# A fused spectral filter and expert layer: sums accumulated in HBM, statistics on ScalarE, and a fixed table of priorities

## The chip, the cores and the metric

The kernel runs on one core of one Trainium2 chip. The metric is the device time of one execution in microseconds (us), lower is better. The engines are named as in the profile: PE (TensorE, matrix products; PEld is its weight load), DVE (VectorE), ACT (ScalarE), POOL (GpSimd), and SP (SyncE), which here issues DMAs.

## What is computed

x has 2048 rows of 576 values. The result is the sum of x and of two branches over its layer norm:

```python
xn = layernorm(x)                                  # per row, eps 1e-5
A  = irfft2(rfft2(xn) * (w_r + 1j * w_i))          # 2-D transform, filter, back
q  = einsum("nd,dhc->nhc", xn, w_q)                # 32 heads, 2 x 128 per head
s1, s2 = q[..., :128] @ k1.T, q[..., 128:] @ k2.T  # 8 scores each
e  = 8 * argmax(s1) + argmax(s2)                   # one of 64 experts per head
B  = sum over heads of gelu(xn . u[e]) * v[e]      # top 1, so its softmax is 1
out = x + A + B
```

## The kernel before

**Tiles.** x is read as 16 tiles of 128 rows; tile t holds the rows n with n mod 16 = t. All matrix products run on PE. Inputs that need more than 16 bits are split into a high and a low 16-bit half and multiplied three times (high by high, high by low, low by high).

**Stages**, in the order in which the program records them:

- `ln` (L631) takes each row's mean and variance: two `bn_stats` of 288 values and one `bn_aggr` per tile on DVE, then the inverse root for a batch of 2 or 4 tiles.
- `folds` (L652) adds and subtracts mirrored halves of the rows (POOL and DVE), and `dft128` (L670) transforms over the 128 rows on PE. ACT copies PSUM as the high half, DVE subtracts for the low half.
- `fold_part` (L753) multiplies the keys into w_q, streamed from HBM in 32 loads of 576 KB through five buffers (tag `w`). `fold_scale` (L773) finds the largest result and `fold_end` (L780) transposes, scales and splits. Only then can the scores be computed.
- For each of 16 frequency groups: `load_w` and `load_s16` load the filter and small transforms, `w_scale` (L734) finds a scale for the filter, `d_fwd` (L897), `s_fwd`, `s_mul` and `s_inv` (L959) transform forward, multiply by the filter and transform back.
- For each of 8 pairs of tiles: `x_t` normalises and transposes x (a transposing DMA), `scores` (L819) computes 512 columns of scores, `route` (L846) and `combine` (L866) find each head's best expert on DVE and build the coefficients (`CAT`).
- For each of 16 tiles: `d_inv` (L990) does the last inverse transform on PE; ACT copies one half out of PSUM, DVE makes a sum and a difference of the halves, POOL puts the row together. `fin` (L1011) does the last product over the rows and the product with the experts' values into one PSUM tile; DVE scales it and adds x, which `load_x` (L540) loaded for two tiles at a time, and SP stores it.

**A maximum over partitions** is `allmax` (L615): PE transposes the column, DVE reduces, DVE puts the maxima on a diagonal (`mxd`), PE multiplies a matrix of ones with the diagonal, DVE clamps from below. It is called for the experts' matrices, for the folded weights and in each `w_scale`.

**The order of the work** is set by a planner in the kernel itself (L226 on). The stages only record operations, each with an estimated duration and its dependencies. The planner first goes backward from the end to get each operation's remaining path (`backward`, L330), then forward in time (`forward`, L350): on each engine it picks, of those that are ready, the one with the highest priority, and it also assigns PSUM banks. Ten such rounds are followed by a search of 1500 tries, in which each stage's priority is shifted at random and the best forecast is kept (`issue`, L443). `bias` values keep early work ahead. Only then are the instructions issued, all of them from one line:

```python
        for i in order:
            for fn, args, kw in ops[i].calls:
                fn(*[x.place() if isinstance(x, _Ps) else x for x in args],
```

That is why every row of the profile has L487; the rows are told apart by the names of their tiles. Each engine runs its own instructions in this fixed order and waits on semaphores for the others. SP's queue is also in order: a load that waits for its buffer holds up what stands behind it. `place` turns a bank number into an address.

Names in the profile: `banks` is PSUM; `Rs`, `A` and `yl` belong to the column transforms; `w` with `KP` to the weight fold; `mm__90` holds the maxima of the folded weights; `wx`, `Wt` and `wa` belong to the filter's scale; `AB` and `ABL` are the spectra; `MU` and `MUL` are the folded weights as the scores use them; `t`, `yh`, `A` and `w` name shared buffers, which the tail uses for the halves, for ACT's copy, for the assembled row and for x.

Of the kernel before, what the change touches and what calls it, by code (L numbers as in the profile page):

```python
# [10 lines left out]
F32 = mybir.dt.float32  # L11
# [124 lines left out]
TRIES, SEED = 1500, 2  # L136
# [87 lines left out]
class _Plan:  # L224
# [7 lines left out]
    def cost(self, eng, m, out, ins, kw):  # L232
# [4 lines left out]
        if eng == "sync":  # L237
            return out.shape[0] * n * size_of(out.dtype) / 400.0 + (2500 if kw.get("transpose") else 0), self.land
# [11 lines left out]
        if eng == "scalar":  # L250
            return (95 if ins[0].space == PSUM else 130) + 0.75 * n + 80 * ptr + 270 * ("accum_out" in kw), 180.0
        if eng == "gpsimd":
# [13 lines left out]
    def add(self, eng, fn, m, args, kw):  # L266
# [7 lines left out]
        port = eng == "gpsimd" and len(ins) > 0 or eng == "vector" and out.space != PSUM and (  # L274
# [75 lines left out]
    def forward(self, prio):  # L350
# [50 lines left out]
        best, stale = dict.fromkeys(free), set(free)  # L401
        while len(order) < len(ops):
# [25 lines left out]
            for v in o.tiles:  # L428
                left[v] -= 1
                end[v] = max(end[v], free[e] + o.lat)  # L430
                if not left[v]:
                    free_at[slot[v]:slot[v] + v.banks] = [end[v]] * v.banks
                    used[v.kind] -= 1
                    stale.add("tensor")
            for k, lat in o.after:
                ready[k] = max(ready[k], free[e] + lat)
# [6 lines left out]
    def issue(self):  # L443
# [16 lines left out]
        for _ in range(ROUNDS):  # L460
# [3 lines left out]
            if best is None or got[0] < best[0]:  # L464
                best = got
                cur = got[0], tail, np.zeros(self.stage + 1)
        rng = np.random.default_rng(SEED)
        for k in range(TRIES):
            f = 1 - k / TRIES
            tail, shift = cur[1], cur[2].copy()  # L470
            pick = rng.random(len(shift)) < (0.02, 0.05, 0.15)[rng.integers(3)]
            shift[pick] += rng.normal(0, 800 + 4000 * f, pick.sum())
            more = 400 * f * f * rng.exponential()
            if k % 40 == 39:
                tail, shift, more = self.backward(got[3]), cur[2], 300
            new = self.forward([t + o.bias + shift[o.stage] for t, o in zip(tail, ops)])
            if new[0] <= cur[0] + more:
                cur, got = (new[0], tail, shift), new
                if new[0] < best[0]:
                    best = new  # L480
# [18 lines left out]
def _body(ctx, tc, nc, plan, a, out):  # L499
# [52 lines left out]
    plan.land = 5600.0  # L552
# [62 lines left out]
    def allmax(src, k, dst):  # L615
# [532 lines left out]
```

## Time and profile before

| | |
|---|---|
| median of 3 runs | 236.74 us (236.53 to 237.49) |
| the profiled execution's own time | 237.5 us |
| its span, from the first to the last instruction | 235.6 us |
| mean granted TensorE clock | 0.986 of full speed |
| moved by DMA | 48.15 MB, 204 GB/s over the span |
| HBM read, written | 38.33 MB, 4.72 MB |

How to read the rows in this document. A row of the busy times gives, for each engine, microseconds in which it worked and the number of instructions; a row of a stretch starts with its limits and length, and ends with the granted clock, the share of time in which the DMA engines were busy and the GB/s. A row of a group names engine, operation, the tile written and the tiles read, the shapes, the count; behind the first bar stand the group's busy time in us and the mean of one instruction in ns, behind the second the idle time just before them and what ended it. In the rows of one tile three durations stand for shortest, median and longest (ns), then the first and last start. A row of the chain gives start, duration, and what ran, on the path that ended last. A DMA row gives count, size and the median us from issue to landing. A row of waits gives us in total, times and the longest.

### The profile page before, as it was taken

To read this page: it belongs to the slowest core of one execution; us is meant where nothing else is said; L and a number is where in the kernel's file an instruction comes from. 1 tells how busy PE (TensorE), PEld (TensorE's weight loads), DVE (VectorE), ACT (ScalarE), POOL (GpSimd) and SP (SyncE) were. 2 spreads that over 40 slices of the span, in tenths; PEclk is the share of its full clock that TensorE was granted. 3 is DMA by queue.
4 is the path that set the end of the run, shared out by engine and by line. 5 is a ranking of instruction groups with operands and counts; after the bars stand their busy time and mean duration, and the time that the engine had idled before them with its cause. 6 is when DMAs were issued, how large, how long until landed. Compare 5 with 4: busy or idle time off the path is not lost.

```text
span 235.6 us, 5937 instructions
## 1 busy us (share of the span) xinstructions
PE 200.0 (85%) x2271; PEld 135.8 (58%) x2271; DVE 204.3 (87%) x446; ACT 125.9 (53%) x287; POOL 134.4 (57%) x183
## 2 busy tenths in 40 slices
PE   0466888998999877899988979689999999999893
PEld 0454657776566545774454566265546778767661
DVE  2789999995999679976499999989999999968992
ACT  2232658989789599989635665256432121223120
POOL 2978768984264446736228886275813746545340
PEclk9997999999999999999999999979999999999999
DMA  6999999999999998466525561330521357662175
GB/s 211 401 403 415 362 334 375 406 349 373 284 338 374 392 251 148 106 164 59 110 53 122 115 134 38 79 59 3 100 59 46 99 156 253 198 203 100 50 245 208
DMA packets 34252, 48.15 MB, mean 204 GB/s; under 512 B 20784, under 2 KB 23088, under 8 KB 33840
## 3 DMA queue, kind: packets, MB, share of 16 engines
q1 hardware_dynamic: 34224, 47.77, 64.7%
q8 instruction: 18, 0.29, 0.6%
q14 instruction: 10, 0.08, 0.1%
HBM read 38.33 MB, written 4.72 MB: 183 GB/s over the span
## 4 chain that ended last, share of the span: by engine, by line
DVE 45%; PE 29%; ACT 9%; issue 8%; DMA 7%; POOL 1%; DVEq 0%; ACTq 0%; POOLq 0%
PE banks L487 29%; DVE w L487 9%; DVE t L487 8%; DVE AB L487 5%; DVE A L487 3%; DVE st L487 3%; DMA Wt<-in_W_dram 3%; DMA w<-in_x_dram 3%; DVE v L487 2%; DVE cw L487 2%; ACT AB L487 2%; DVE mx L487 2%; DVE ABL L487 2%; DMA XN<-in_x_dram 2%; DVE rr L487 2%
## 5 line engine op out<-in xcount | busy, mean ns | idle before, releaser
L487 POOL TENSOR_TENSOR A<-t 128x145 f32<-128x145 f32 (+3 forms) x56 | 38.4, 706 | 18.9 <-DVE t L487 12.2
L487 PE MATMUL banks<-MU,xT 128*128 128x512 f16 x192 | 46.0, 380 | 0.0
L487 PE MATMUL banks<-c,AB 128*128 128x145 f16 (+1 forms) x384 | 35.6, 228 | 0.7 <-DVE AB L487 0.7
L487 PEld LDWEIGHTS <-AB 128*128 128x128 f16 x384 | 31.6, 121 | 6.7 <-issue 4.3
L487 PE MATMUL banks<-Rs,A 128*128 128x128 f32 x128 | 20.5, 310 | 16.1 <-ACT Rs L487 11.8
L487 POOL TENSOR_TENSOR y<-t,t 128x289 f32<-128x289 f32 x32 | 21.7, 700 | 21.2 <-DVE t L487 20.8
L487 PEld LDWEIGHTS <-xT 128*128 128x128 f16 x224 | 19.8, 97 | 23.7 <-issue 4.1
L487 POOL TENSOR_TENSOR yh<-y,yh 128x578 f16<-128x578 f32 x16 | 20.6, 1285 | 16.7 <-ACT yh L487 12.9
L487 PEld LDWEIGHTS banks<-Rs,A 128*128 128x128 f32 x128 | 17.7, 214 | 21.1 <-ACT Rs L487 14.1
L487 POOL TENSOR_TENSOR t<-XN 128x289 f32<-128x289 f32 x32 | 24.5, 782 | 8.2 <-DMA XN<-in_x_dram 3.8
L487 DVE TENSOR_TENSOR AB<-banks,AB 128x512 f16<-128x512 f32 x32 | 21.6, 676 | 5.2 <-ACT AB L487 2.7
L487 DVE SCALAR_TENSOR_TENSOR t<-banks,wx,Wt 128x578 f32<-128x578 f32 x32 | 24.9, 807 | 0.4 <-PE banks L487 0.3
L487 POOL TENSOR_TENSOR hl<-XN,hl 128x576 f16<-128x576 f32 x16 | 20.0, 1254 | 8.0 <-ACT hl L487 8.0
L487 PE MATMUL banks<-c,ABL 99*128 99x289 f16 (+1 forms) x64 | 18.7, 292 | 5.6 <-DVE t L487 2.7
L487 ACT ACTIVATE yh<-banks,sc 128x290 f32<-128x290 f32 x16 | 8.0, 503 | 27.9 <-PE banks L487 23.9
L487 PE MATMUL banks<-A,c 128*128 128x288 f32 x64 | 21.6, 419 | 0.5 <-DVE t L487 0.5
L487 PE MATMUL banks<-w,KP 128*32 128x288 f32 x256 | 21.2, 428 | 0.0
L487 ACT ACTIVATE ABL<-banks 99x256 f16<-99x256 f32 x32 | 12.1, 378 | 16.6 <-PE banks L487 15.8
L487 ACT ACTIVATE AB<-banks 128x512 f16<-128x512 f32 x32 | 18.9, 590 | 0.1
L487 PE MATMUL banks<-s,yh 64*128 64x128 f16 x384 | 14.5, 222 | 4.9 <-ACT yh L487 1.9
L487 DVE TENSOR_TENSOR ABL<-banks,ABL 33x256 f16<-33x256 f32 x32 | 13.0, 405 | 6.3 <-ACT ABL L487 3.2
L487 PEld LDWEIGHTS <-yh 64*128 64x128 f16 x384 | 11.6, 97 | 9.6 <-issue 3.5
(104 smaller groups left out, 416.5 us busy)
## 6 DMA issues: line engine op xcount, KB each, us to landing
w<-in_wq_dram SPq DMA_DIRECT2D x32, 576.0 KB, 6.2
Wt<-in_W_dram SPq DMA_DIRECT2D x16, 289.0 KB, 5.4
w<-in_x_dram SPq DMA_DIRECT2D x8, 576.0 KB, 4.3
out_dram<-w SPq DMA_DIRECT2D x16, 288.0 KB, 2.7
XN<-in_x_dram SPq DMA_DIRECT2D x3, 1282.0 KB, 12.7
s<-in_s_dram SPq DMA_DIRECT2D x16, 192.0 KB, 3.1
XN<-in_x_dram SPq DMA_DIRECT2D x2, 641.0 KB, 5.0
c<-in_c_dram SPq DMA_DIRECT2D x1, 868.5 KB, 7.5
```

What stands on the lines that cost most here:

```text
L487: fn(*[x.place() if isinstance(x, _Ps) else x for x in args], **{k: x.place() if isinstance(x, _Ps) else x for k, x in kw.items()})
```

## The change

Four things are changed together, and the order of all instructions with them.

1. **The table.** The 1500 tries are dropped. A table `SHIFT` of one number per stage is written into the kernel and added to the priorities before one last forward pass. Some of the planner's estimates differ: loads early in the program count 3000 ns to landing where it was 5600, transposing DMAs 1200; a DMA issued from POOL is known; a queue of SP that is long busy adds 2600 ns; stages of the frequency groups get a small bias of 1e4.
2. **Maxima.** In `allmax` the diagonal is gone: the matmul takes the maxima, repeated along the free dimension with stride zero, as the stationary operand and the identity as the moving one. A factor can be multiplied in the clamp, which removes a DVE multiply in `w_scale` and in `fold_scale`.
3. **Statistics.** For tiles 5, 7, 9, 11, 13 and 15, `ln` takes them on ACT: one pass with an accumulator gives the negative mean (scaled), a second the mean square of the difference; POOL scales the mean.
4. **The tail.** For tiles 4, 5, 8 and 9, `d_inv` copies both halves out of PSUM on ACT, and POOL makes the difference that DVE made. For tiles 2, 3, 6 and 7 x isn't loaded: two DMAs on SP copy it from HBM to the output in HBM, `fin` lets ACT scale the PSUM tile into SBUF, and a DMA issued from POOL adds that to the output. In the new order the two copies stand among the last third of the loads of w_q.

```diff
-TRIES, SEED = 1500, 2
+SHIFT = (
+    4944, 32508, -18408, -5252, -68789, 83522, -16944, 5194, 4161, -48778, 60478, -11552, -28309,
...
+)
...
-        rng = np.random.default_rng(SEED)
-        for k in range(TRIES):
...
+        best = self.forward([t + o.bias + SHIFT[o.stage] for t, o in zip(cur[1], ops)])
...
+            lag = 0.0
+            if e == "sync":
+                if t0 > full[1]:
+                    full[0] = t0
+                full[1] = free[e] + 300
+                lag = 2600.0 if t0 - full[0] > 1500 else 0.0
...
-    plan.land = 5600.0
+    plan.land = 3000.0
...
-    def allmax(src, k, dst):
+    def allmax(src, k, dst, up=None):
...
-        dg = T([4, 4], F32, "mxd", 4)
-        V.tensor_scalar(dg[:k, :k], idn[:k, :k], m[:k, 0:1], None, op0=OP.mult)
-        P.matmul(p[:, 1, :k], ones[:k, :], dg[:k, :k], start=True, stop=True)
-        V.tensor_scalar(dst, p[:, 1, :k], 1e-10, None, op0=OP.max)
+        P.matmul(p[:, 1, :k], m[:k, 0:1].to_broadcast([k, 128]), idn[:k, :k], start=True, stop=True)
+        if up is None:
+            V.tensor_scalar(dst, p[:, 1, :k], 1e-10, None, op0=OP.max)
+        else:
+            V.tensor_scalar(dst, p[:, 1, :k], 1e-10, up, op0=OP.max, op1=OP.mult)
...
+    SA = (5,7,9,11,13,15)
...
+            if t + i in SA:
+                j, b = T([128, D], BF, "wa", 1), rr[:, 3, t + i:t + i + 1]
+                A.activation(j, XN[:, t + i, 64:64 + D], AF.Copy, scale=-1.0 / 13824, accum_out=b)
+                A.activation(j, XN[:, t + i, 64:64 + D], AF.Square, scale=1.0 / 24, bias=b, accum_out=mv[:, i, 1:2])
+                G.tensor_scalar(mv[:, i, 0:1], b, -24.0, None, op0=OP.mult)
+                continue
...
-        allmax(wm[:, g:g + n], n, wx[:, 0, g:g + n])
+        allmax(wm[:, g:g + n], n, wx[:, 0, g:g + n], 4096.0)
         V.reciprocal(wx[:, 1, g:g + n], wx[:, 0, g:g + n])
-        V.tensor_scalar(wx[:, 1, g:g + n], wx[:, 1, g:g + n], 2.0 ** -12, None, op0=OP.mult)
...
-        allmax(mm_[:, 4:5], 1, sc[:, 3:4])
+        allmax(mm_[:, 4:5], 1, sc[:, 3:4], 2.0 ** -10)
         V.reciprocal(sc[:, 7:8], sc[:, 3:4])
-        V.tensor_scalar(sc[:, 7:8], sc[:, 7:8], 1024.0, None, op0=OP.mult)
...
+    RES = dict.fromkeys((2,3,6,7))
...
+    def copy_x(t, n):
+        Q.dma_start(os[:, t:t + n, :], xs[:, t:t + n, 64:64 + D])
+        for i in range(t, t + n):
+            RES[i] = len(plan.ops) - 1
...
+    EG = (4,5,8,9)
...
+        if t in EG:
+            es = T([128, 2, 290], F32, "qs", 2, "yh")
+            A.activation(es, p[:, :, 0:290], AF.Copy, scale=sc[:, 12:13])
+            qs = es[:, :, 145:290]
...
+        if t in EG:
+            G.tensor_tensor(eo[:, :, 288:144:-1], es[:, :, 0:144], qs[:, :, 0:144], op=OP.subtract)
+        else:
+            V.scalar_tensor_tensor(eo[:, :, 288:144:-1], p[:, :, 0:144], sc[:, 12:13], qs[:, :, 0:144],
+                                   op0=OP.mult, op1=OP.subtract)
...
-        x = xin[t // 2][:, t % 2]
+        x = xin[t // 2][:, t % 2] if t not in RES else T([128, D], F32, "xo", 5, "w")
...
+        if t in RES:
+            A.activation(x.rearrange("p (h d) -> p h d", h=2), p[:, :, :288], AF.Copy, scale=sc[:, 11:12])
+            plan.gate = {RES[t]}
+            G.dma_start(os[:, t, :], x, accum_op=OP.add)
+            plan.gate = set()
+            return
...
+    for t in range(0, 16, 2):
+        if t in RES:
+            copy_x(t, 2)
+    for t in (0, 2):
+        if t not in RES:
+            load_x(t)
...
-        if t % 2 == 0 and t and t + 2 < 16:
+        if t % 2 == 0 and t and t + 2 < 16 and t + 2 not in RES:
             load_x(t + 2)
```

More of the change, by code (lines that the diff above doesn't have):

```diff
@@ L400, in forward @@
         order, start = [], [0.0] * len(ops)
-        best, stale = dict.fromkeys(free), set(free)
+        best, stale, full = dict.fromkeys(free), set(free), [0.0, 0.0]
         while len(order) < len(ops):
@@ L465, in issue @@
                 best = got
-                cur = got[0], tail, np.zeros(self.stage + 1)
-        rng = np.random.default_rng(SEED)
-        for k in range(TRIES):
[L469 to L480, printed above, removed]
+                cur = got[0], tail
+        best = self.forward([t + o.bias + SHIFT[o.stage] for t, o in zip(cur[1], ops)])
         _, order, slot, start = best
```

26 lines of the change are left out of this document (15 added, 11 removed), and 18 rows, old and new, of the table SHIFT.

## The prediction

> **What bounds the kernel now.** I read the busy shares of the engines first, then the busy times of three stretches, cut where the work changes.
>
> ```profile
> span 235.6 us, 5937 instructions
> ## 1 busy us (share of the span) xinstructions
> PE 200.0 (85%) x2271; PEld 135.8 (58%) x2271; DVE 204.3 (87%) x446; ACT 125.9 (53%) x287; POOL 134.4 (57%) x183
> ```
>
> DVE (VectorE) and PE (TensorE) are both near full. The share over the whole span hides which one ends last, so the stretches matter: up to 54 us the column transforms (`ln`, `folds`, `dft128`), 54 to 106 us the rest of the weight fold and the chain to the first scores, 106 to 232 us everything else.
>
> ```profile
> core 0: us, PE busy (x) PEld busy (x) DVE busy (x) ACT busy (x) POOL busy (x), PEclk, DMA share, GB/s
> 4.00:54.00 50.00, 37.86 (x319) 28.76 (x323) 46.54 (x136) 28.54 (x79) 40.73 (x66) 0.97 0.99 380
> 54.00:106.00 52.00, 45.55 (x787) 32.08 (x780) 42.54 (x88) 44.73 (x95) 25.85 (x29) 1.00 0.92 267
> 106.00:232.00 126.00, 116.60 (x1170) 74.97 (x1168) 114.43 (x216) 51.32 (x114) 67.35 (x84) 0.99 0.42 111
> ```
>
> In the first stretch DVE is the bound (46.5 of 50 us) with POOL (GpSimd) next. In the second no engine is full; DMA is the busiest (0.92). In the third PE idles 126 - 116.6 = 9.4 us and DVE 11.6 us: two engines at 91 to 93% that hand work to each other. The granted clock is 0.97 to 1.00 throughout, so it plays no part.
>
> **The change, part by part.** *First stretch: six tiles' statistics go from DVE to ScalarE.*
>
> ```profile
> 0.00:54.00 54.00, 13.82 (x48) 0.97 0.96 363
> ```
>
> ```profile
> L487 ACT ACTIVATE wa<-Wt 128x578 bf16<-128x578 f32 x16 | 10.9, 682 | 2.5 <-DMA Wt<-in_W_dram 2.3
> ...
> L487 ACT ACTIVATION_READ_ACCUMULATOR wa<-Wt 128x1 f32 x16 | 3.1, 195 | 0.0
> ...
> L487 POOL TENSOR_SCALAR rr<-mv 128x2 f32<-128x2 f32 x2 | 0.5, 270 | 0.2
> ```
>
> The first row is DVE's time on the statistics tile `st`: 13.82 us for 16 tiles, so six tiles give 13.82 x 6/16 = 5.2 us back. ScalarE gets 12 passes with an accumulator. None over `XN` stands in the trace; the nearest rows are the same kind over 578 columns of `Wt` (682 + 195 ns), so 12 x 0.88 = 10.5 us. ScalarE was busy 28.54 of 50, and becomes 39.1. POOL gets six one-column multiplies by the 0.27 us row, 1.6 us: 40.73 becomes 42.3. DVE also loses one diagonal of `allmax` here (0.80 us, a row quoted below), and comes to 46.54 - 5.2 - 0.8 = 40.5. So POOL is late next, with 42.3. Today the fullest engine of this stretch is 50 - 46.5 = 3.5 us short of its length; with the same loss POOL's bound is 45.8, a gain of 4.2 us. The bounds are 0 (ScalarE, where the statistics now stand in line before PSUM evictions, makes PE wait for as much) and 6.0 (all of DVE's saving). I take **-4**. If POOL's cover is gone too, because it waits for ScalarE's accumulators, this term vanishes.
>
> *Second stretch: shorter `allmax`, and two copies of x from HBM to HBM.* `allmax` loses the DVE instruction that built a diagonal (`mxd`), and its broadcast matmul now takes the maxima as a stationary operand repeated with stride zero. `w_scale` and `fold_scale` lose a multiply, since the factor rides in the clamp.
>
> ```profile
> 0.00:54.00 54.00, 0.38 (x2) 0.29 (x2) 0.80 (x1) 0.97 0.96 363
> 54.00:106.00 52.00, 2.27 (x12) 1.76 (x12) 2.83 (x6) 1.00 0.92 267
> 106.00:180.00 74.00, 0.76 (x4) 0.59 (x4) 1.69 (x2) 0.98 0.38 78
> ```
>
> ```profile
> 89.71 1.10 DVE mxd L487
> ...
> 91.48 0.76 DVE wx L487 x2
> 92.24 0.65 DVE mm__90 L487
> ...
> 94.29 1.12 DVE wx L487
> ```
>
> ```profile
> w<-in_x_dram SPq DMA_DIRECT2D x8, 576.0 KB, 4.3
> ```
>
> The first three rows are `mxd` by stretch (third number, DVE): nine instructions, 5.3 us. Off the chain they are worth nothing in this stretch, where DVE has 9.5 us to spare. But the chain that leads to the first scores runs through them: `mm__90`, the maximum of the folded weights, stands behind an `mxd` of 1.10 us and the `wx` pair of 0.76, and a `wx` multiply of 1.12 follows. These were long because they waited inside DVE: the shortest `wx<-wx` is 0.15 us (row below). Taking the three out shortens the chain by 1.10 + 0.6 + 1.12 = 2.8 us; between 0 (PE has other work at that point in any case) and 2.8.
>
> The copies carry 2 x 576 KB = 1.18 MB. In the instruction order they stand between the last third of the 32 weight loads, where before there was no x traffic; the two `load_x` that they replace stood in the tail, where DMA is idle. At the 380 GB/s of the first stretch they push the remaining weight loads back by 1.18/380 = 3.1 us. Bounds: 0, as SP spends much of its time waiting for PE to release weight buffers (74.0 us in 35 waits over the span, quoted below) so that the loads have slack; and 6.2, if a copy costs as a read and as a write. I take 3.1, so this stretch comes to 3.1 - 2.8 = **+0.3**.
>
> A page speaks against the copies. The Trainium skill, "DMA: Bandwidth & Descriptors", section "Where 436 GB/s comes from", puts a limit of about 358 GB/s on HBM traffic of a core, and a copy inside HBM would count twice: an estimate by that page is 2.36 MB / 358 GB/s = 6.6 us instead of 3.1, and a sum 3.5 us later. The trace does not show that limit: 380 GB/s stand in the row of the first stretch.
>
> *Third stretch: less DVE work per tile, and sums added in HBM.*
>
> ```profile
> L487 DVE SCALAR_TENSOR_TENSOR w<-banks,sc,w 128x576 f32<-128x576 f32 x16 | 12.5, 806 | 2.3 <-PE banks L487 1.3 <-DMA w<-in_x_dram 1.0
> ...
> L487 ACT ACTIVATE yh<-banks,sc 128x290 f32<-128x290 f32 x16 | 8.0, 503 | 27.9 <-PE banks L487 23.9 <-DVE v L487 3.3 <-ACT MT L487 0.7
> L487 DVE SCALAR_TENSOR_TENSOR t<-banks,sc,yh 128x288 f32<-128x288 f32 x16 | 8.0, 502 | 0.0
> ...
> L487 POOL TENSOR_TENSOR A<-t 128x288 f32<-128x288 f32 x8 | 6.2, 773 | 0.1
> ...
> L487 ACT ACTIVATE MT<-banks 128x576 f32<-128x576 f32 x4 | 2.6, 650 | 0.2 <-PE banks L487 0.2
> ```
>
> ```profile
> L487 DVE TENSOR_SCALAR wx<-wx x7: 151/170/1190, 53.6 to 140.8; 128x2 f32<-128x2 f32 x6, 128x4 f32<-128x4 f32 x1
> ```
>
> DVE loses: four final sums, 4 x 0.81 = 3.2 us; four subtractions of `d_inv`, 4 x 0.50 = 2.0; two `mxd`, 1.7; two `wx` multiplies, between 0.3 and 2.4 by the min and max of their row, say 1.2. Together 8.1 us, and DVE comes from 114.4 to 106.3. PE's matmuls are the same, and in both instruction orders the same 96 column-transform, 128 fold, 168 `d_fwd`, 192 `s_fwd` and 252 `s_inv` matmuls stand ahead of the first scores. So PE's 116.6 us remain, and become the bound: its idle 9.4 us is all that can be won here. ScalarE gets four evictions (0.65) and four wider ones (about 0.65 for 0.50, by the same row), 3.2 us on 51 of 126. POOL gets four subtractions (3.1 us) and four DMA issues on 67 of 126; both are covered. With DVE 8.1 us lighter, and with the last scores moved ahead in the order (behind three `d_inv` and half a final sum, where nine `d_inv` and six final sums stood ahead of them), the tail holds little but PE work. I take 6 of the 9.4, leaving 3.4 us, as much as the fullest engine of the first stretch loses. Bounds 0 (PE's waits are for hand-offs between ScalarE, DVE and POOL, which remain) and 9.4. Term **-6**.
>
> *The accumulating DMA* is in no trace here. Its landing is bounded by the quickest output store (2.1 us) and by the slowest bulk load, 12.7 us for 1282 KB of `XN`:
>
> ```profile
> XN<-in_x_dram SPq DMA_DIRECT2D x3, 1282.0 KB, 12.7
> ```
>
> ```profile
> L487 SPq DMA_DIRECT2D out_dram<-w x16: 332/344/927, 188.9 to 232.6; - x16
> ...
> DMA to landing us min/median/max: 2.1/2.7/6.9
> ```
>
> ```profile
> SPq L487 <- PE banks L487: 74.0, 35, 12.6
> ```
>
> I take twice the median store, 5.4 us, since it has to read what it adds to. Who waits for it: SP's load of x for tile 10 (its buffer is that of tile 2's sum) and for tile 12 (tile 3's). SP works in order, so the stores of tiles 4 and 5 and the load of tile 8 stand behind those waits. The stores run from 188.9 to 232.6 us, 2.7 us a tile; tile 8 comes five tiles after tile 3, 13.6 us. Take off the eviction (0.65), an issue on POOL (0.3 to 0.9 by SP's rows), one on SP (0.3) and the 4.3 us load: 13.6 - 0.65 - 0.6 - 0.3 - 4.3 = 7.7 us are free. At 5.4 it costs nothing.
>
> *The table of priorities* takes the place of the planner's search; I price its order only through the stretches above. The end stays: the last store is issued at 232.6 and lands 2.7 us later.
>
> **The sum**: -4 + 0.3 - 6 = -9.7 us on a span of 235.6, so 226. The profiled execution took 237.5, which becomes 227.8; the median of the runs is 236.74, 0.76 lower, so **227** us.
>
> **The rivals.**
> 1. *The copies cost both ways* (chance 0.18). The second stretch then gets +6.2 - 2.8 = +3.4, and a later start of the scores also leaves DVE less room ahead of them, so that the third gives 3 rather than 6: -4 + 3.4 - 3 = -3.6, 233. For it speaks DMA's share of 0.92 to 0.99 up to 106 us; against it, SP's waits for PE. This is the page's rule above, priced by rows.
> 2. *Everything is recovered* (0.14): -6.0, -2.8 with the copies hidden, -9.4: -18.2, so 218.5; anything under 222 counts here.
> 3. *The time stays* (0.06), 236 to 238. What DVE no longer does turns into waits: ScalarE evicts late in the first stretch, and PE's 9.4 us are hand-offs. Speaking for it: POOL, at 40.7 of 50, allows little even now.
> 4. *Slower, through the accumulating DMA* (0.10). If its landing takes L us, L - 7.7 of it delays the load of tile 8, and DVE, which works in order, holds up the `d_inv` steps queued behind that final sum. Past L = 7.7 + 9.7 = 17.4 us the kernel is slower than before; at L = 22 it takes 241. Against it: the slowest bulk load took 12.7 us. The Trainium skill, "SBUF — State Buffer", section "SBUF: two separate sides", says that a POOL-issued DMA starves while DVE holds the port that the two share, and the section after it gives 3.1 us against 0.62; by that page an estimate is 2.5 us more per DMA, so 7.9 us where I have 5.4, which would use up the slack and no more. No trace of before shows a DMA from POOL.
>
> **How the numbers follow.** My forecast, 222 to 231, has 0.52; the rivals the chances above, rival 1 reaching from 231 to 235.5. Measurement can tell about 0.5% (1.2 us) from no change. Faster by over 0.5%: 0.52 + 0.18 + 0.14 = 0.84; within: 0.06; slower: 0.10. The range goes from 220, which takes in half of rival 2, to 236, which leaves out the slow case and part of the unchanged: 0.52 + 0.07 + 0.18 + 0.04 = 0.81.
>
> **What would show it.** Right: DVE's busy time near 185 us instead of 204; no `mxd` row; the last column-transform matmul 3 to 5 us before 54 us; the first scores near 102 us; PE busy nearly without gaps from there; accumulating DMAs landing in 3 to 8 us. Wrong: a first stretch as long as before with PE waiting for ScalarE; the last weight load later than before; final sums waiting for `w<-in_x_dram`; ScalarE's passes over `XN` far from 0.88 us.

## The result, and the profile after

The changed kernel takes **239.59 us** (median of 4 runs, 238.85 to 239.88) where the kernel before takes 236.63 on the same chip: the ratio is 1.0114, with a 95% interval from 1.0079 to 1.015. The forecast was 227 with a range from 220 to 236, so the sign was wrong, and 12.6 us are to be explained. Part of it is a wait that can be removed, and without it the changed kernel is some 2% faster than the kernel before.

The profiled execution took 239.45 us, its span 237.6. First the busy times of its page:

```profile
span 237.6 us, 5938 instructions
PE 199.7 (84%) x2271; PEld 135.2 (57%) x2271; DVE 190.7 (80%) x403; ACT 136.7 (58%) x315; POOL 142.1 (60%) x197
```

DVE lost 13.6 us of work, ScalarE gained 10.8, POOL 7.7, as the change intends. The three stretches (PE, PEld, DVE, ACT, POOL, then clock, DMA share, GB/s):

```profile
4.00:54.00 50.00, 36.64 (x329) 26.59 (x329) 41.87 (x115) 36.55 (x105) 42.57 (x72) 1.00 1.02 391
54.00:106.00 52.00, 47.18 (x788) 33.80 (x781) 39.10 (x83) 46.36 (x97) 28.22 (x30) 0.97 0.95 282
106.00:232.00 126.00, 114.25 (x1157) 73.93 (x1155) 107.56 (x198) 52.47 (x114) 70.82 (x91) 0.96 0.41 99
```

DVE is lighter in each of them (41.87 for 46.54, 39.10 for 42.54, 107.56 for 114.43), and the third stretch is the worse for it: PE works 114.25 of 126 us where it worked 116.60. Two milestones say where the time went. In the timeline of PE (start, duration) of the kernel before, the last column transform and the first scores:

```profile
53.25 0.60 PE L487 MATMUL banks<-Rs,yl 128*99 128x128 f32 x4
...
105.87 2.76 PE L487 MATMUL banks<-MU,xT 128*128 128x512 f16 x12
```

and in that of the changed kernel:

```profile
53.09 0.60 PE L504 MATMUL banks<-Rs,yl 128*99 128x128 f32 x4
...
104.33 2.76 PE L504 MATMUL banks<-MU,xT 128*128 128x512 f16 x12
...
218.15 1.30 PE L504 MATMUL banks<-A,c 128*128 128x288 f32 x2 [3.98 <-DVE w L504]
...
219.72 1.17 PE L504 MATMUL banks<-A,c 128*128 128x288 f32 x2
```

The column transforms end at 53.7 instead of 53.9 us and the scores start 1.5 us earlier. From there on it loses 3.5 us, for the span is 2.0 longer. But each of these times is that of one execution. before_xn (an experiment below) issues the same instructions in the same order up to the scores and starts them at 104.28, as early as the changed kernel. The difference opens near 81 us, where PE in the profiled execution of the kernel before waited for a load of `s`:

```profile
81.75 1.68 PE L487 MATMUL banks<-A,s 64*64 64x289 f16 x47 [0.84 <-DMA s<-in_s_dram]
```

```profile
104.28 2.76 PE L532 MATMUL banks<-MU,xT 128*128 128x512 f16 x12
```

The first row is the kernel before, the second before_xn. So a gain ahead of the scores isn't shown; counted from before_xn, whose span is 234.7, the changed kernel is level up to them and loses 2.9 us behind them. The last rows of the changed kernel above show the largest single loss: PE stands for 3.98 us at 218.15, waiting for DVE, and the products behind it run at half speed (1.30 and 1.17 us for pairs of matmuls that take 0.65 to 0.75 elsewhere). The chain of the changed kernel names what DVE waits for:

```profile
202.57 0.75 ACT w L504
...
203.62 0.88 POOL out_dram L504
...
209.99 7.11 DMA w<-in_x_dram
...
217.19 0.83 DVE w L504
...
218.15 14.73 PE banks L504 x98
```

The load of x for tiles 8 and 9 is issued at 209.99 and lands 7.11 us later; DVE has been waiting for it, with the `d_inv` steps of the next tiles behind it. DVE's row and that of ScalarE in the timelines, with the idle time in brackets, say how it got late:

```profile
206.43 1.20 DVE L504 TENSOR_REDUCE cw<-w 128x32 f32<-128x1024 bf16 x1
...
217.19 0.82 DVE L504 SCALAR_TENSOR_TENSOR w<-banks,sc,w 128x576 f32<-128x576 f32 x1 [5.49 <-DMA w<-in_x_dram]
```

```profile
202.57 0.74 ACT L504 ACTIVATE w<-banks,sc 128x576 f32<-128x576 f32 x1 [4.37 <-DVE cw L504]
```

```profile
202.37 0.39 SPq L504 DMA_DIRECT2D w<-in_x_dram  x1
...
209.03 0.39 SPq L504 DMA_DIRECT2D w<-in_x_dram  x1
209.52 0.42 SPq L504 DMA_DIRECT2D out_dram<-w  x1
209.99 0.42 SPq L504 DMA_DIRECT2D w<-in_x_dram  x1
```

ScalarE stood idle for 4.37 us before it could scale tile 3, since its tile of the sum (`xo`) is one of the five `w` buffers, and routing of the seventh pair (`cw`) was still reading it; with a buffer of its own (x_in_w below) the same step ran at 200.00. So the accumulating DMA of tile 3 was issued at 203.62. SP's load at 209.03 (tiles 12 and 13) goes into that buffer and had to wait for its landing, and the load of tiles 8 and 9 stood behind it in SP's queue. That load had a second holder: in the rotation of the five buffers it comes to the one that routing of the eighth pair uses, which is read until 207.63 (the first row of DVE). An estimate from these rows: the accumulating DMA and the queue held the load up for 2.4 us (207.63 to 209.99), and the other 3.1 of DVE's 5.49 us would have been there without them.

### The profile page after: what moved, and what is told of

It is laid out like the page before. It is cut to its first block, busy times and chain, and to the rows that moved or that the text cites. A ratio compares the mean times of both kernels' runs of the same rounds, so it can differ in the third digit from the quotient of the medians.

```text
span 237.6 us, 5938 instructions
## 1 busy us (share of the span) xinstructions
PE 199.7 (84%) x2271; PEld 135.2 (57%) x2271; DVE 190.7 (80%) x403; ACT 136.7 (58%) x315; POOL 142.1 (60%) x197
## 4 chain that ended last, share of the span: by engine, by line
PE 42%; DVE 28%; ACT 11%; issue 7%; DMA 7%; POOL 3%; DVEq 0%; SPq 0%; ACTq 0%; POOLq 0%
PE banks L504 42%; DVE w L504 5%; DVE t L504 4%; DVE A L504 3%; DMA w<-in_x_dram 3%; DVE AB L504 3%; DVE st L504 2%; ACT AB L504 2%; DMA w<-in_wq_dram 2%; DVE rr L504 2%; ACT XN L504 2%; DVE ABL L504 2%; DMA XN<-in_x_dram 2%; POOL yh L504 1%; DVE MU L504 1%
## 5 line engine op out<-in xcount | busy, mean ns | idle before, releaser
L504 PE MATMUL banks<-MU,xT 128*128 128x512 f16 x192 | 47.4, 390 | 0.0
L504 POOL TENSOR_TENSOR A<-t 128x145 f32<-128x145 f32 (+3 forms) x56 | 36.6, 678 | 10.3 <-DVE t L504 5.2
L504 PEld LDWEIGHTS <-xT 128*128 128x128 f16 x224 | 20.3, 99 | 25.9 <-issue 6.4
L504 PEld LDWEIGHTS <-AB 128*128 128x128 f16 x384 | 32.2, 123 | 4.5 <-issue 3.0
L504 PE MATMUL banks<-Rs,A 128*128 128x128 f32 x128 | 19.8, 298 | 16.0 <-ACT Rs L504 11.9
L504 POOL TENSOR_TENSOR yh<-y,yh 128x578 f16<-128x578 f32 x16 | 21.5, 1346 | 14.4 <-ACT yh L504 14.3
L504 POOL TENSOR_TENSOR y<-t,t 128x289 f32<-128x289 f32 x32 | 22.6, 727 | 12.1 <-DVE t L504 11.4
L504 PEld LDWEIGHTS banks<-Rs,A 128*128 128x128 f32 x128 | 16.7, 201 | 22.0 <-ACT Rs L504 13.5
L504 PE MATMUL banks<-A,c 128*128 128x288 f32 x64 | 22.7, 438 | 4.8 <-DVE w L504 4.0
L504 ACT ACTIVATE yh<-banks,sc 128x290 f32<-128x290 f32 (+1 forms) x16 | 8.9, 564 | 19.4 <-PE banks L504 15.4
```

The source lines that it names most:

```text
L504: fn(*[x.place() if isinstance(x, _Ps) else x for x in args], **{k: x.place() if isinstance(x, _Ps) else x for k, x in kw.items()})
```

## The experiments

**How they are made.** Instead of planning, each kernel issues its operations in a fixed order (`ORDER`) with fixed PSUM banks (`SLOT`), taken from one of the two kernels. An operation that the other kernel does not have stands where the one stood that it replaces. So an edit can be undone without moving the rest.

```diff
-        best = self.forward([t + o.bias + SHIFT[o.stage] for t, o in zip(cur[1], ops)])
-        _, order, slot, start = best
...
+        order = ORDER
+        for v, k in zip(self.tiles, SLOT):
+            v.slot = k
```

Most of them also take the buffers out of the question: `XN`, the buffer of the layer norm's input, is free in the tail, and x and the sums go there (`_xn` in the names).

```diff
-        xin[t // 2] = T([128, 2, D], F32, "xin", 5, "w")
+        xin[t // 2] = XN[:, t:t + 2, 64:64 + D]
...
-        x = xin[t // 2][:, t % 2] if t not in RES else T([128, D], F32, "xo", 5, "w")
+        x = xin[t // 2][:, t % 2] if t not in RES else XN[:, t, 64:64 + D]
```

My theory was that the tail's wait and the new order lose what the edits gain; the rival, that hand-offs set the pace and the edits are worth nothing.

### Buffers: after_xn, x_in_w, sums_in_w

**after_xn** is the changed kernel with the diff above.

> The changed kernel in its own order; only x of the tail (load_x) and ScalarE's scaled tiles of the sums lie in XN, which is free by then, instead of in the five w buffers that routing still holds. Theory A (the loss is in the tail: the load of tiles 8 and 9 waits for a buffer and behind loads that wait for the accumulating DMAs, DVE stands 5.5 us, PE 4.0 us, and matmuls at a lowered clock follow): 239.6 less 4 to 6, so 233.5 to 235.5, with no wait of DVE for w<-in_x_dram over 1 us. Theory B (the edits are worth nothing, since hand-offs between ScalarE, DVE and POOL set the pace, and the tail's wait only shows what is lost already): 237.5 to 239.5.

Measured: 231.94 us, ratio to the kernel before 0.9797 (0.9717 to 0.9877), 7.7 us less than the changed kernel. In PE's timeline the scores start when they did in the changed kernel, the longest wait of PE from 200 us on is 0.61 us, and the last product starts at 225.94 us where it started at 233.19:

```profile
53.58 0.60 PE L541 MATMUL banks<-Rs,yl 128*99 128x128 f32 x4
...
104.18 2.76 PE L541 MATMUL banks<-MU,xT 128*128 128x512 f16 x12
...
202.34 0.28 PE L541 MATMUL banks<-c,ABL 99*128 99x290 f16 x1 [0.61 <-DVE XN L541]
...
225.94 0.41 PE L541 MATMUL banks<-vS,MT 128*128 128x288 f16 x2
```

The wait of theory A is the loss that the buffers cause, and removing it gives more than the 4 to 6 us that I expected. The other two runs take one half of the diff each. **x_in_w** moves only the sums:

```diff
-        x = xin[t // 2][:, t % 2] if t not in RES else T([128, D], F32, "xo", 5, "w")
+        x = xin[t // 2][:, t % 2] if t not in RES else XN[:, t, 64:64 + D]
```

> The changed kernel with only ScalarE's scaled tiles of the sums moved to XN; x of the tail still goes through the five w buffers. No load then waits for an accumulating DMA, but the loads of tiles 10 and 12 take buffers that routing of the last two pairs holds, and the load of tile 8 stands behind them in SP's queue. Theory A1 (the landing of the accumulating DMAs is what holds up tile 8's load, as rival 4 has it): 231 to 233.5, like after_xn. Theory A2 (routing holds the buffers, the accumulating DMAs only add to it): 236 to 239, with DVE still waiting 3 us or more for w<-in_x_dram.

Measured: 234.63 us (ratio 0.9942, 0.9903 to 0.998). It lies between the theories: no load waits for an accumulating DMA now, and 5.0 us are gone, but DVE still waits for x. The sums no longer take part in the rotation, so the load of tiles 8 and 9 has a free buffer; the load ahead of it in SP's queue, that of tiles 12 and 13, waits for routing of the last pair until 207.6 us:

```profile
206.37 1.20 DVE L541 TENSOR_REDUCE cw<-w 128x32 f32<-128x1024 bf16 x1
...
214.86 0.82 DVE L541 SCALAR_TENSOR_TENSOR w<-banks,sc,w 128x576 f32<-128x576 f32 x1 [3.85 <-DMA w<-in_x_dram]
```

```profile
207.60 0.90 SPq L541 DMA_DIRECT2D w<-in_x_dram  x2
```

**sums_in_w** moves only x:

```diff
-        xin[t // 2] = T([128, 2, D], F32, "xin", 5, "w")
+        xin[t // 2] = XN[:, t:t + 2, 64:64 + D]
```

> The other half: x of the tail goes to XN, ScalarE's scaled tiles of the sums stay in the five w buffers, so ScalarE still waits near 202 us for routing to give one back (4.4 us in the changed kernel). No load waits for anything in the tail. Theory A (the x loads are what costs): 231 to 233, like after_xn. If ScalarE's late eviction, with the d_inv copies behind it, costs by itself: 234 to 237.

Measured: 231.9 us (0.9801, 0.9747 to 0.9855), as good as after_xn. My expectation had one point wrong: with x gone, the sums come to other buffers of the five, which are free early, and ScalarE's wait is gone too, so a late eviction by itself was not tried. Sums alone in the five buffers cost nothing, x alone costs 2.7 us (routing's hold), and both together another 5.0 (late evictions and the accumulating DMAs in front of the loads, which these runs do not separate).

### Edits and order apart: before_xn, order_xn, edits_xn

**before_xn** is the kernel before, in its order, with x in XN (the first half of the diff); **order_xn** has no edit, but the changed kernel's order; **edits_xn** has all edits, but the order of the kernel before. The first entries of the table of the last, against after_xn:

```diff
-    18, 13, 0, 8, 9, 10, 11, 12, 6, 7, 1, 2, 3, 19, 39, 20, 40, 22, 23, 41, 21, 24, 43, 26, 25, 33, 27, 331, 28,
+    18, 13, 0, 12, 8, 9, 10, 11, 6, 7, 1, 2, 3, 19, 39, 20, 40, 22, 23, 41, 21, 24, 43, 26, 25, 32, 27, 331, 28,
```

> The kernel before in its own order, only x of the tail loaded into XN. DVE waits for x 1.0 us in all in the kernel before, so all theories expect 235.5 to 237; it is what edits_xn and order_xn are compared with.

> No edit of the change, but in its instruction order, the instructions that it dropped at the place of those that stood for them, and x of tiles 2, 3, 6 and 7 loaded next to the loads of tiles 0 and 4; x of the tail in XN. Theory C: slower than before_xn by 2 to 6 us, with the wait of PE near 142 to 148 us that the changed kernel has. Theory B: within 1.5 us of before_xn.

> All edits of the change, but in the instruction order of the kernel before (an instruction that is new stands where the one that it replaces stood; the two copies stand behind the same weight loads as in the changed kernel); x of the tail in XN as in after_xn. Theory C (the edits are a gain, the new order is the loss): 229 to 233, at least 2 us less than after_xn. Theory B: 235.5 to 238, the same as before_xn. Theory D (the edits only pay in an order made for them): slower than before_xn.

| | order of the kernel before | new order |
|---|---|---|
| without the edits | before_xn 236.16 (1.0032, 0.9977 to 1.0087) | order_xn 241.99 (1.0215, 1.0134 to 1.0297) |
| with the edits | edits_xn 240.83 (1.0161, 1.0091 to 1.0231) | after_xn 231.94 (0.9797, 0.9717 to 0.9877) |

Theory B falls, and so does C, which I held: the edits lose 4.7 us in the old order and win 10.0 in the new one, while the new order alone costs 5.8. It is theory D, order and edits only pay together. The part before the scores shows it already. The last column transform ends at 53.6 us in before_xn, 56.5 in edits_xn, 57.3 in order_xn and 54.2 in after_xn (start and 0.60 us of the row that the timelines above show). All of the 4.2 us by which after_xn is ahead of before_xn lie behind the scores, which start at 104.18 and 104.28. The PSUM banks go with the order in these runs, so "order" means both; no run separates them.

### The edits one at a time, in the new order: stats_xn, maxima_xn, loads_xn, split_xn

Each is after_xn with one edit undone:

```diff
-    SA = (5,7,9,11,13,15)
+    SA = ()
```

> after_xn (231.9 us) with the statistics of the six tiles back on DVE (SA empty), each where the pass of ScalarE stood; all else as in after_xn. The prediction's first term (DVE sets the pace of the first stretch): 4 us slower, 235 to 237. Against it, the traces: the last column transform ends at 53.6 to 54.2 us with and without the moved statistics, POOL works 41 to 43 of the first 54 us and each transform waits for a product that POOL begins: within 1 us of after_xn.

```diff
-        P.matmul(p[:, 1, :k], m[:k, 0:1].to_broadcast([k, 128]), idn[:k, :k], start=True, stop=True)
+        dg = T([4, 4], F32, "mxd", 4)
+        V.tensor_scalar(dg[:k, :k], idn[:k, :k], m[:k, 0:1], None, op0=OP.mult)
+        P.matmul(p[:, 1, :k], ones[:k, :], dg[:k, :k], start=True, stop=True)
...
+        V.tensor_scalar(wx[:, 1, g:g + n], wx[:, 1, g:g + n], 2.0 ** -12, None, op0=OP.mult)
...
+        V.tensor_scalar(sc[:, 7:8], sc[:, 7:8], 1024.0, None, op0=OP.mult)
```

> after_xn with the maxima as before: the diagonal mxd and the multiply behind the reciprocal are back, nine and eight small instructions of DVE. The prediction's second term and its share of the third: 2.8 us on the chain to the first scores and up to 2.9 later, 3 to 5 us slower, 235 to 237. If the chain to the first scores has other waits beside it: 0.5 to 2 us slower, 232.5 to 234.

```diff
-    RES = dict.fromkeys((2,3,6,7))
+    RES = {}
```

> after_xn without the copies and the accumulating DMAs: x of tiles 2, 3, 6 and 7 is loaded into XN (beside the loads of tiles 0 and 4), DVE scales and adds, SP stores. The prediction priced the copies at +3.1 us and the four final sums that DVE lost at some 2.4 (its share of the third term): 0 to 1 us faster. If the copies are hidden behind PE's work: 2 to 3 us slower, 234 to 235. If the copies cost both ways (rival 1): 2 to 4 us faster.

```diff
-    EG = (4,5,8,9)
+    EG = ()
```

> after_xn with the differences of d_inv of tiles 4, 5, 8 and 9 back on DVE (EG empty). The prediction's share: 2.0 us of DVE at 6 parts of 8.1, 1.5 us slower, 233.5. If these steps have slack in the new order: within 0.7 us of after_xn.

| undone | median us, ratio to before | against after_xn |
|---|---|---|
| stats_xn | 236.37, 0.9971 (0.9935 to 1.0006) | +4.4 |
| maxima_xn | 235.97, 0.9963 (0.9928 to 0.9998) | +4.0 |
| loads_xn | 231.79, 0.978 (0.9719 to 0.9842) | -0.2 |
| split_xn | 234.02, 0.9869 (0.9814 to 0.9923) | +2.1 |

Together 10.4 us, about what all of them undone cost (order_xn, 10.0). The statistics (4.4 us for 4), the maxima (4.0 for 2.8 and some 2 of the third stretch) and the split of `d_inv` (2.1 for 1.5) are each worth about what the prediction said; the copies and the accumulating DMAs, taken together with the four sums that they take from DVE, are worth nothing either way. These four ran on another chip than after_xn; by the ratios the prices are 4.1, 3.9, -0.4 and 1.7, and the interval of split_xn overlaps that of after_xn, so the last is the least sure. An order made with the edits may punish their absence, so these prices hold for this order. PE's timeline in stats_xn:

```profile
56.80 0.60 PE L541 MATMUL banks<-Rs,yl 128*99 128x128 f32 x4
...
107.42 2.76 PE L541 MATMUL banks<-MU,xT 128*128 128x512 f16 x12
```

Against after_xn, the column transforms end 3.2 us later, and the scores start 3.2 us later. In maxima_xn they end at the same time and the scores start at 107.15, 3.0 later.

### What limits the first and second stretch: folds_xn, head_old, mix_xn, maxima_old

**folds_xn** takes work from POOL in the first stretch:

```diff
-    FF, DV = {}, range(1, 16, 2)
+    FF, DV = {}, (1, 2, 3, 5, 6, 7, 9, 10, 11, 13, 14, 15)
```

> after_xn with one subtraction per tile of the tiles 2, 6, 10 and 14 (folds, about 0.7 us each on POOL) moved from POOL to DVE, where the statistics made room. If POOL sets the pace of the first stretch now: the last column transform ends 2 to 2.8 us earlier than 54.2 and the time falls by 1.5 to 2.8 us, 229 to 230.5. If hand-offs between POOL, DVE and ScalarE set it: within 1 us of after_xn, or slower.

Measured: 232.74 us (0.9812, 0.9751 to 0.9873), and the transforms end at 54.3. POOL works 2.3 us less in the stretch, and nothing follows: it is not POOL alone.

**head_old** is stats_xn, in whose table the operations of the first stretch stand in the order of the kernel before:

```diff
-    18, 13, 0, 8, 9, 10, 11, 12, 6, 7, 1, 2, 3, 19, 39, 20, 40, 22, 23, 41, 21, 24, 43, 26, 25, 33, 27, 331, 28,
+    18, 13, 0, 12, 8, 9, 10, 11, 6, 7, 1, 2, 3, 19, 39, 20, 40, 22, 23, 41, 21, 24, 43, 26, 25, 32, 27, 331, 28,
```

> stats_xn (236.4 us; statistics on DVE) with the instructions of the first stretch (ln, folds, dft128 and the first half of fold_part, all engines but SP) in the order of the kernel before, the rest as it was. If the new order costs some 3 us in the first stretch, so that the statistics only make up for it: the last column transform ends near 54 us instead of 57.4 and the time is 232 to 233.5. If the loads (SP's queue stays in the new order) or something else makes the stretch longer: 235.5 to 237.

Measured: 234.06 us (0.9898, 0.9861 to 0.9935), and the column transforms end at 54.2: the old order needs no moved statistics for that. But the scores start at 106.56 us, 2.4 later than in after_xn, so only 2.3 of the 4.4 us come back. **mix_xn** goes the other way: with all edits, it takes the first stretch from the order of search3_xn (below), whose transforms end early.

```diff
-    18, 13, 0, 8, 9, 10, 11, 12, 6, 7, 1, 2, 3, 19, 39, 20, 40, 22, 23, 41, 21, 24, 43, 26, 25, 33, 27, 331, 28,
+    18, 13, 0, 8, 9, 10, 11, 12, 6, 7, 1, 2, 3, 19, 39, 20, 40, 22, 23, 41, 21, 24, 43, 26, 33, 27, 331, 28, 14,
```

> after_xn (231.9 us) with the instructions up to the last column transform in the order of search3_xn (loads of that part too; last column transform near 51.4 us there), and those behind it in the table's order. If the first stretch sets when the scores can start: first scores 2 to 3 us before 104.2 and 229 to 230. If ScalarE, which works 47 of the 52 us behind it, absorbs it: first scores at 103.5 to 104.5 and 231 to 233.

Measured: 231.65 us (0.9807, 0.9743 to 0.987). In PE's timeline:

```profile
50.93 0.60 PE L541 MATMUL banks<-Rs,yl 128*99 128x128 f32 x4
...
103.68 2.76 PE L541 MATMUL banks<-MU,xT 128*128 128x512 f16 x12
```

The transforms end 2.7 us earlier than in after_xn, the scores start 0.5 us earlier, which is no more than the scatter: six runs with one and the same order up to the scores (the changed kernel, after_xn, x_in_w, sums_in_w, split_xn and act_first_xn) start them between 103.75 and 104.36. The stretches of after_xn suggest why; ScalarE is the fourth engine in the row:

```profile
84.00:94.00 10.00, 8.77 (x168) 6.81 (x168) 7.46 (x21) 10.00 (x23) 5.56 (x7) 1.00 0.91 172
94.00:106.00 12.00, 10.73 (x164) 8.22 (x157) 10.19 (x19) 11.60 (x27) 8.36 (x9) 1.00 0.74 147
```

ScalarE works 10.00 of 10 us and then 11.60 of 12, right up to the first scores, as in mix_xn (10.00 and 11.61). So it can absorb what is gained ahead of it. This is read off the rows: in mix_xn a load of w_q that lands at 80.70 stands ahead of ScalarE in the chain, and no run makes either of them lighter. **maxima_old** has one edit alone, the shorter maxima, in the order and with the buffers of the kernel before:

```diff
-        dg = T([4, 4], F32, "mxd", 4)
-        V.tensor_scalar(dg[:k, :k], idn[:k, :k], m[:k, 0:1], None, op0=OP.mult)
-        P.matmul(p[:, 1, :k], ones[:k, :], dg[:k, :k], start=True, stop=True)
+        P.matmul(p[:, 1, :k], m[:k, 0:1].to_broadcast([k, 128]), idn[:k, :k], start=True, stop=True)
```

> The kernel before, in its own order and with its own buffers, with one edit alone: the shorter maxima (17 small instructions of DVE fewer). The prediction's second term: 2.8 us on the chain to the first scores, 233 to 234.5 against 236.5. If the old order hides it: 235.5 to 237.

Measured: 234.61 us (0.9916, 0.9883 to 0.9949). The time falls by about 2 us. The scores start at 103.69 us, 2.2 ahead of the profiled execution of the kernel before but only 0.6 ahead of before_xn, so where the 2 us are won stays open. An edit that only removes work needs no new order.

### One wait of ScalarE: act_first_xn

Near 142 us ScalarE waits 3.03 us for `mx` of DVE, with `yh` behind it, for which PE waits. `act` (ScalarE) and `mx` read the same PSUM tile, and the one that is later in the order waits for the other. The edit moves `act` of the pairs 2 and 6 forward in `ORDER`; for pair 6:

```diff
-    936, 931, 1111, 1003, 1112, 856, 1136, 1006, 1004, 857, 1005, 1137, 1121, 937, 1138, 932, 938, 1052, 1139,
+    936, 931, 1111, 1003, 1112, 856, 1136, 1004, 1006, 857, 1005, 1137, 1121, 937, 1138, 932, 938, 1052, 1139,
```

> after_xn with one kind of instruction moved: for the score pairs 2 and 6 ScalarE's gelu (act) stands ahead of DVE's maximum (mx) over the same PSUM tile in the order, as it does for the six other pairs; for these two it stood behind. If the order of the two readers alone makes ScalarE wait (3.0 us at 142 us, with yh behind it and PE waiting 3.5 us for yh): PE's waits near 146 and 147.5 us go and the time falls by 1.5 to 3.5 us, 228.5 to 230.5. If PE makes up for that wait later anyway: within 0.7 us of after_xn.

Measured: 232.32 us (0.9807, 0.9759 to 0.9855), no gain, though ScalarE runs `act` at 142.30 and `yh` at 142.83. PE in after_xn and then in act_first_xn:

```profile
146.15 0.28 PE L541 MATMUL banks<-s,yh 64*128 64x128 f16 x4 [2.46 <-ACT yh L541]
147.50 1.17 PE L541 MATMUL banks<-s,yh 64*128 64x128 f16 x20 [1.07 <-POOL yh L541]
```

```profile
146.29 1.46 PE L541 MATMUL banks<-s,yh 64*128 64x128 f16 x24 [2.42 <-DVE ABL L541]
```

The same 2.4 us are there with another name: DVE, which is busy with routing all the time (8.00 of 8 us from 142 on), comes to `ABL` no earlier.

### Other orders for the same edits: search2_xn, search3_xn

The program of after_xn, ordered by the search of the kernel before with two seeds:

```diff
-        best = self.forward([t + o.bias + SHIFT[o.stage] for t, o in zip(cur[1], ops)])
+        rng = np.random.default_rng(SEED)
+        for k in range(TRIES):
...
```

> The program of after_xn, its order found by the search of the kernel before (1500 tries, seed 2, the changed estimates) instead of the table. If any order made for the edits keeps their gain of some 10 us over the kernel before less what each order loses: 229 to 233. If the table is what the gain hangs on: 235 to 240. The planner's own forecast says 219.7 us for this order and 241.2 for the table's; if it ranks orders rightly, this run is over 10 us faster than after_xn.

> The same with seed 3, to see how far two orders of one program lie apart (the planner's forecast: 221.5 us, 1.8 us over that of search2_xn). If orders found with the same estimates are alike: within 1.5 us of search2_xn. If an order alone moves the time by several us: 2 to 6 us apart.

Measured: search2_xn 0.9858 (0.9755 to 0.996), search3_xn 233.77 us, 0.988 (0.9805 to 0.9955); the runs of search2_xn scatter from 232.3 to 239.2, so I use its ratio alone, and the seeds can't be told apart. Both are faster than the kernel before, and after_xn is not surely faster than they are. So the edits do not hang on the table. The planner's forecasts (219.7 and 221.5 us, and 241.2 for the table's order) do not rank the orders: the one that it likes least has the lowest median. In search3_xn the transforms end at 51.4 us, 2.5 ahead of the kernel before, and the scores start at 103.15.

## Why the prediction was wrong, point by point

**The tail's slack: failed.** "Take off the eviction (0.65), an issue on POOL (0.3 to 0.9 by SP's rows), one on SP (0.3) and the 4.3 us load: 13.6 - 0.65 - 0.6 - 0.3 - 4.3 = 7.7 us are free." The distance was that of the old order, 13.6 us, and the rest took every buffer as free and the load at its median. Even the kernel before had no such slack: the row of the final sums in the prediction has 1.0 us of waiting for `w<-in_x_dram`. In the new order the DMA of tile 3 is issued at 203.62, after ScalarE's wait for the buffer, and DVE is ready for the first sum of tiles 8 and 9 at 211.7: 8.1 us. What has to fit into them is 5.4 us until SP's load for tile 12 can go (209.03), 0.96 of SP and 7.11 of the load, 13.5 us, and 5.4 us are missing, which is DVE's wait. With no accumulating DMA at all some 3 us would be left, by an estimate: the load's own buffer is free at 207.63, and 7.11 us behind that is 214.7. x_in_w, where no load waits for such a DMA, has 3.85. The landing itself was well priced; the issues of the accumulating DMAs and their median us to landing:

```profile
out_dram<-w POOLq DMA_DIRECT2D x4, 288.0 KB, 5.0
```

5.0 us for 5.4. So rival 4 had the place, but not the point from which it decides: it asked for a landing of 17.4 us, and the wait came about at 5.0, through an eviction that was late, buffers that routing held and a load that took 7.11 us for 4.3. With the loads in XN it is gone, and 7.7 us with it.

**The order: failed.** "The table of priorities takes the place of the planner's search; I price its order only through the stretches above." That set it to nothing. Without the edits it costs 5.8 us (order_xn), and the edits in the old order cost 4.7 (edits_xn). The terms could only be added to the kernel before if its order stayed good for the changed work.

**First stretch, -4 forecast, -0.2 measured.** The prices were near: DVE lost 4.7 us of work (for 6.0), the passes of ScalarE took 0.88 and 0.96 us with the reading of the accumulator.

```profile
L504 ACT ACTIVATE wa<-XN,rr 128x576 bf16<-128x576 f32 x6 | 4.6, 770 | 0.0
L504 ACT ACTIVATE wa<-XN 128x576 bf16<-128x576 f32 x6 | 4.1, 680 | 0.0
...
L504 ACT ACTIVATION_READ_ACCUMULATOR wa<-XN 128x1 f32 x6 | 1.2, 196 | 0.0
L504 ACT ACTIVATION_READ_ACCUMULATOR wa<-XN,rr 128x1 f32 x6 | 1.2, 193 | 0.0
```

Undone in the new order they cost 3.2 us at the last column transform and 4.4 of time. But this order needs them to reach the 54 us that the old order reaches without, and what another order gains there (mix_xn) is lost again before the scores. That last part, as far as the rows go, is the step "in the second no engine is full; DMA is the busiest": over 52 us ScalarE's 44.7 look harmless, but in the kernel before it works 9.57 of 10 and 11.29 of 12 us between 84 and 106:

```profile
84.00:94.00 10.00, 7.25 (x112) 4.71 (x112) 8.87 (x20) 9.57 (x21) 5.04 (x6) 1.00 1.07 174
94.00:106.00 12.00, 10.83 (x206) 9.22 (x195) 10.28 (x24) 11.29 (x26) 6.65 (x9) 1.00 0.56 133
```

The stretch was cut too wide to show it.

**Second stretch, +0.3 forecast, -1.4 measured, about 0 against before_xn.** The maxima are borne out at the first scores in the new order alone, with 3.0 us for 2.8; in the old one they are worth 2 us of time, of which 0.6 us at the scores are seen against before_xn. The copies were priced too high: without them the scores start at 103.84 us, within the scatter of the runs that have them, and the time is the same, so their lower bound, 0, fits (loads_xn takes out the sums with them). (They stand behind the 17th and the 23rd of the 32 weight loads; "the last third" was too late.) Rival 1, that they cost both ways, did not happen, and the limit of about 358 GB/s that the Trainium skill gives for a core's HBM traffic ("DMA: Bandwidth & Descriptors", section "Where 436 GB/s comes from") is not what this case shows: the changed kernel's DMA moves 391 GB/s over the first stretch. That section works the limit out as half of what two cores share, and here one core runs.

**Third stretch, -6 forecast, +3.5 measured, -3.5 in after_xn** (+2.9 and -4.2 against before_xn). The split of `d_inv` was worth 2.1 us for my 1.5, the four sums nothing for my 2.4 (loads_xn). The part that did not come, in after_xn, stands at places like 142 to 148 us, where DVE is still full (act_first_xn): taking 7 of 114 us from DVE over the whole stretch does not empty it where PE waits for it.

**The clock "plays no part": wrong for the changed kernel.** Its granted clock is 0.97 and 0.96 in the second and third stretch, and twelve products take 4.37 us for 2.76 (last section). What that costs in all, no run separates: its 2271 matmuls are busy for 199.7 us, those of after_xn for 196.1, and those of the kernel before for 200.0.

Of the signs that the prediction named, `mxd` is gone, the accumulating DMAs land within 3 to 8 us and DVE is busy for 190.7 us (for 185); of those against it, the final sum that waits for `w<-in_x_dram` came.

What stays open: why the new order without the statistics is 3.4 us slower in the first stretch (folds_xn excludes POOL alone), and how much of the 4.9 us between after_xn and the forecast a better order could still get. The best versions (mix_xn, loads_xn, sums_in_w and after_xn, 231.65 to 231.94 us, ratios 0.978 to 0.981) can't be told apart.

## What to carry to other kernels

Where an order is planned by hand or by machine, an edit and the order it runs in are one change: hold the order fixed and undo one part at a time before putting a price on either. When a buffer gets a new user, follow its whole line, from who holds it now to which loads wait for it and what stands behind them in the queue; a slack that was read off the old order does not carry over. Before a milestone that comes 1 or 2 us earlier is called a gain, see how far executions of the same instructions scatter. Cut the stretches short enough to see an engine that is full only just ahead of the step that everything waits for.

## What the runs showed of the hardware

**The clock was lower behind three waits of PE.** The page of the changed kernel (40 slices of 5.9 us, tenths of full speed):

```profile
PEclk9999999999997999999999997699999999998899
```

The low slices are the 13th (71 us on), the 25th and 26th (143 us on) and the 37th and 38th (214 us on). In each PE had just waited, by its timeline:

```profile
73.07 0.85 PE L504 MATMUL banks<-s,yh 64*128 64x128 f16 x24 [1.69 <-DVE t L504]
...
146.30 0.40 PE L504 MATMUL banks<-s,yh 64*128 64x128 f16 x4 [2.46 <-ACT yh L504]
147.66 1.25 PE L504 MATMUL banks<-s,yh 64*128 64x128 f16 x20 [0.96 <-POOL yh L504]
149.48 4.37 PE L504 MATMUL banks<-MU,xT 128*128 128x512 f16 x12
```

and 3.98 us at 218.15. The twelve products at 149.48 take 4.37 us where the same twelve took 2.76 at 104.33, and those behind 218.15 ran at half speed for some 2.9 us (rows above). In x_in_w the wait before the same product is shorter, and the product runs at full speed:

```profile
215.82 0.72 PE L541 MATMUL banks<-A,c 128*128 128x288 f32 x2 [2.46 <-DVE w L541]
```

The Trainium skill, "TensorE: Matmul & The Clock Gate", section "What's actually happening", has the clock at half after an idle window of about 3.4 us whose place is not tied to the kernel. The half speed agrees; the waits of 1.7 and 2.5 us are shorter than that window and went with a lower clock all the same. Their length alone does not decide: 2.46 us did so at 146 us and not at 215.8 in x_in_w, and the wait near 73 us stands in all six runs that share this order, 1.68 or 1.69 us long, while the granted clock from 70 to 80 us is 0.83 in three of them (the changed kernel, x_in_w, act_first_xn) and 1.00 in the others. In the traces' clock records every half-speed stretch that ends before the span does lasts 3.4 us or twice that. Both fit a window whose place is free; no run here sets the wait by itself.

**An accumulating DMA from POOL holds POOL for 1 us.** The group of its issues:

```profile
L504 POOL DMA_DIRECT2D out_dram<-w x4 | 3.7, 994 | 6.7 <-ACT w L504 6.2 <-DVE pw L504 0.6
```

994 ns each, above the 0.3 to 0.9 us that I took from SP's stores. Here POOL had the time.

**The load of tiles 8 and 9 was slow to land.** It took 7.1 us, against a median of 4.1 for the six loads of x, with another load of 576 KB and a store issued within 1 us ahead of it.
